# The first weights are loaded on another queue, and the list schedule is given other durations

## The chip, the cores and the metric

The kernel runs on one core of a Trainium2 chip. The metric is the time of one execution on the device, in microseconds (us); lower is better.

## What is computed

Sliding-window attention (window 64) on 4 batches of 8 heads, 576 positions and 64 dimensions, then two gated layers on the resulting 2304 tokens of 512 features. The weights are float64, everything else float32.

```python
scores = where(0 <= i - j < 64, q @ k.T / sqrt(64), -1e9)
x = softmax(scores) @ v               # 2304 tokens x 512
h = x @ w_in                          # 512 -> 2048
x = (h * clip(h + 3, 0, 6) / 6) @ w_out
h = x @ w2_in
out = leaky_relu(h, 0.01) @ w2_out    # 2304 x 512
```

## The kernel before

TensorE (PE) does every product. For the two layers each operand is split into a high and a low part, and three matmuls (high·high, high·low, low·high) add up in one PSUM bank, so a block of 128 x 512 costs three matmuls. The tokens are cut into five blocks (four of 512, one of 256), the hidden 2048 features into 16 slices of 128, f. For every (layer, block, f), `st_h` makes `h` (line 576; 12 matmuls) and `st_y` adds its product with the second weight to the four banks `y` (line 635; 12 matmuls).

**Weights.** `convert` brings one piece of weights (128 rows of 512 float64 values, 512 KB) into `st` and makes two tiles of it, `w0h`/`w0l` (first weight) or `w1h`/`w1l` (second). ScalarE (ACT) writes the absolute value `ca` (line 343) and the scaled low word `cr` (354); VectorE (DVE) clamps and shifts `ca` in two steps (331), puts sign and exponent back (350), adds `cr` (304); ACT copies the sum to the high tile (294) and DVE subtracts for the low tile (304). That is five DVE operations and three ACT operations for each of 64 pieces.

**Attention.** 20 items, each one or two query blocks. `st_S` writes the mask into the banks `y` (early items) or `a` by a matmul with the identity (line 453) and adds the products of `kt` and `qt` (466). DVE takes the maximum (`nb`, 425 and 426), ACT the exponentials (`s`, 414), DVE sums and inverts (435, 421, 422), GpSimd (POOL) scales (305). `st_P` transposes on PE (483, into banks `h`), ACT copies (`pt`), `st_V` multiplies by `v` (514), ACT copies into `xa`. The first 512-token block needs nine items before its first `h`; its tokens are then split by ACT into `xs0h`..`xs3h` and by DVE into `xs0l`..`xs3l`.

**What sets the order.** The kernel first records every operation with the engines that could do it, a duration for each, and what it reads and writes. `Order.run` then plays list scheduling forward and backward six times, keeps the shortest plan and issues the operations in its order. Durations come from the helpers `act`, `dve`, `pool` and `pe`, DMAs from `load`; every load is issued on the queue of SyncE (SP). Outside that list stands a preamble: `zero` (DVE memset, and an ACT activation that brings in the table for exp), the identity `ident_r` and the mask `mask_r`, made by POOL in a buffer and cast by DVE (lines 674 and 685). The list does not hold these, though line 453 needs both. The engines run their own instructions strictly in order, and wait for each other by semaphores.

Of the kernel before, what the change touches and what calls it, by code (L numbers as in the profile page):

```python
# [10 lines left out]
U32 = mybir.dt.uint32  # L11
# [204 lines left out]
def swa_relu6_leaky_kernel(ctx: ExitStack, tc: tile.TileContext, q, k, v, w_in, w_out, w2_in, w2_out, out):  # L216
# [14 lines left out]
    nc = tc.nc  # L231
    B, _, NP, S = k.shape
    NT, DM = out.shape
    DFF = w_out.shape[0]
    P = 128
# [9 lines left out]
    SCALE = 1.0 / float(DM // (2 * NP)) ** 0.5  # L245
    MASKED = -(2.0 ** 30)
    APART = lambda n, e: n < 5
    EARLY = 9

    blocks = [(sum(SIZES[:i]), n) for i, n in enumerate(SIZES)]  # L250
# [22 lines left out]
    op = od.op  # L273
# [8 lines left out]
        return ("ACT", 0.19 + n * 0.00083, fn)  # L282

    def dve(n, fn, fast=False):
        return ("DVE", 0.15 + n * (0.00052 if fast else 0.00104), fn)

    def pool(n, fn):
        return ("POOL", 0.2 + n * 0.0024, fn)

    def pe(t, fn):  # L290
        return ("PE", t, fn)
# [13 lines left out]
        p = pool(n, lambda: nc.gpsimd.tensor_tensor(out=dst(), in0=a(), in1=b(), op=alu))  # L305
        return (d, p) if last else (p, d)

    def load(bytes_, dst, src, writes):
        op([("SP", 0.62, lambda: nc.sync.dma_start(out=dst(), in_=src))], writes=writes)  # L309
        op([("DMA", bytes_ / 3.6e5, lambda: None)], writes=writes, delay=2.0)  # L310


# [2 lines left out]
    parts = {}  # L315

    def convert(layer, f, part):
        src = ((w_in, w_out), (w2_in, w2_out))[layer][part]
        st = buf("st", [P, DM, 2], U32, bufs=3)
        a = buf("ca", [P, DM], U32)  # L320
        r = buf("cr", [P, DM], U32)
        hi = buf(f"w{part}h", [P, DM], F32R, bufs=RING)
        lo = buf(f"w{part}l", [P, DM], F32R, bufs=RING)
        parts[layer, f, part] = hi, lo
        load(
            P * DM * 8, lambda: st().rearrange("p n t -> p (n t)"),
            src[f * P:(f + 1) * P, :].bitcast(U32), [st],
        )

        def ts(dst, src, s1, s2, op0, op1=None):  # L330
            return dve(DM, lambda: nc.vector.tensor_scalar(  # L331
                out=dst(), in0=src(), scalar1=s1, scalar2=s2, op0=op0, **({"op1": op1} if op1 else {})
            ), True)

        def high():
            return st()[:, :, 1]

        def af():
            return a().bitcast(F32)


        op([
            act(DM, lambda: nc.scalar.activation(out=af(), in_=high().bitcast(F32), func=AF.Abs)),
            ts(a, high, 0x7FFFFFFF, None, ALU.bitwise_and),
        ], [st], [a])
        op([ts(af, af, EXP_LO, EXP_HI, ALU.max, ALU.min)], [a], [a])

        op([ts(a, a, 3, 0x3FFFFFFF, ALU.logical_shift_left, ALU.bitwise_and)], [a], [a])

        op([dve(DM, lambda: nc.vector.scalar_tensor_tensor(  # L350
            out=a(), in0=high(), scalar=0xC0000000, in1=a(), op0=ALU.bitwise_and, op1=ALU.bitwise_or
        ))], [a, st], [a])

        op([act(DM, lambda: nc.scalar.activation(
            out=r(), in_=st()[:, :, 0], func=AF.Copy, scale=2.0 ** -29
        ))], [st], [r])
        op(tensor_tensor(DM, a, a, r, ALU.add, ADD_BY_VECTOR), [a, r], [a])
        op(copy(DM, hi, af, True), [a], [hi])
        op(tensor_tensor(DM, lo, af, lambda: hi().bitcast(F32), ALU.subtract), [a, hi], [lo])
# [83 lines left out]
    def st_S(n, pps):  # L443
        b, us = items[n]
        t = (us[0] - 1) // 2 if us[0] else 0
        if (b, t) not in tiles:
            load_tile(b, t)
        x, y = tiles[b, t]
        L = P if us[0] else W

        early = n < EARLY
        for pp in pps if early else ():
            op([pe(0.25, lambda pp=pp: nc.tensor.matmul(
                pp()[:, 0:NP * L].rearrange("p (c l) -> p c l", c=NP), ident_r,
                mask_r[:, P - L:P].unsqueeze(1).to_broadcast([P, NP, L]), start=True, stop=True,
                skip_group_check=True,
            ))], writes=[pp])

        def fn():
            for c in range(NP):  # L460
                for e in range(2):
                    r = slice(e * W, (e + 1) * W)
                    for j in range(len(us)):
                        part, pp = (j, pps[e]) if us[0] else (e, pps[0])
                        i = j + (1 if us[0] and not t else 0)
                        nc.tensor.matmul(  # L466
                            pp()[part * W:(part + 1) * W, c * L:(c + 1) * L], y()[r, i, c, :],
                            x()[r, c, j * W:j * W + L], start=not early,
                            stop=True, skip_group_check=early,
                        )  # L470

        op([pe(0.25 + NP * 0.222 * L / P, fn)], [x, y], pps)
        probs[n] = [softmax(L, pp, early, early and APART(n, e)) for e, pp in enumerate(pps)]

    def st_P(n, pps):
        L = P if items[n][1][0] else W
        pts[n] = []
        for (s, sv), pp in zip(probs.pop(n), pps):
            pt = buf("pt", [P, NP * P], bufs=3)

            def fn(sv=sv, pp=pp):
                for c in range(NP):
                    nc.tensor.transpose(pp()[0:L, c * P:(c + 1) * P], sv()[:, c, :], ident)  # L483

            op([pe(NP * 0.11, fn)], [s], [pp])
            op(copy(NP * P, lambda pt=pt: pt()[0:L], lambda pp=pp: pp()[0:L]), [pp], [pt])
            pts[n].append(pt)

# [10 lines left out]
    def st_V(n, po):  # L499
        b, us = items[n]  # L500
        L = P if us[0] else W
        pt = pts.pop(n)
        vs = []
        for i in us:
            vv = od.slot("v", sb, [P, DM], F32, 2, HOMES["v"])
            load(L * DM * 4, lambda vv=vv: vv()[0:L], v[b, (i + 1) * W - L:(i + 1) * W, :], [vv])
            vs.append(vv)

        def fn():
            for j, vv in enumerate(vs):  # L510
                for c in range(NP):
                    for e in range(2):
                        x, i = (pt[e], j) if us[0] else (pt[0], e)
                        nc.tensor.matmul(  # L514
                            po()[e * W:(e + 1) * W, (j * NP + c) * W:(j * NP + c + 1) * W],
                            vv()[0:L, (2 * c + e) * W:(2 * c + e + 1) * W],
                            x()[0:L, c * P + i * W:c * P + (i + 1) * W], start=True, stop=True,
                        )

        op([pe(0.15 + len(us) * NP * 0.125, fn)], [*vs, *pt], [po])  # L520
        n0 = b * NQ + us[0]
        bb, o = block_of(n0 * W)
        if len(us) == 2 and block_of((n0 + 1) * W)[0] != bb:
            groups = [((0,), bb, o), ((1,), *block_of((n0 + 1) * W))]
        else:
            groups = [(tuple(range(len(us))), bb, o)]
        for js, bb, o in groups:
            m = len(js)
            op(copy(
                m * NP * W,  # L530
                lambda bb=bb, o=o, m=m: xa[bb].rearrange("p (c l) -> p c l", c=NK)[:, :, o:o + m * W].rearrange(
                    "p c (j w) -> p j c w", j=m),
                lambda js=js, m=m: po()[:, js[0] * NP * W:(js[0] + m) * NP * W].rearrange(
                    "p (j c w) -> p j c w", j=m, c=NP),
            ), [po], [("x", n0 + j) for j in js])
# [18 lines left out]
    gs, xs, ys = {}, {}, {}  # L554
# [7 lines left out]
    def st_h(idx):  # L562
        layer, b, f, first, last = steps[idx]
        n = blocks[b][1]
        if first:
            names = x_names(layer, b)
            src = xb if layer else xa
            for c in range(NK):
                xs[c] = split(n, f"xs{c}", lambda c=c: xc(src, b, c), [names[c]] if layer else names)
        hi, lo = parts[layer, f, 0]  # L570
        ph = bank("h", 2)
        for c in range(NK):
            def fn(c=c, x=xs[c]):
                cs = slice(c * P, (c + 1) * P)
                for m, (wt, xt) in enumerate(((hi, x[0]), (lo, x[0]), (hi, x[1]))):
                    nc.tensor.matmul(  # L576
                        ph()[:, 0:n], wt()[:, cs], xt()[:, 0:n],
                        start=(c == 0 and m == 0), stop=(c == NK - 1 and m == 2),
                    )
            op([pe(3 * (0.0132 + n / 2400), fn)], [hi, lo, *xs[c]], [ph])  # L580
        r = buf("r", [P, 512])
        gh = buf("gh", [P, 512], F32R)
        gl = buf("gl", [P, 512], F32R)
# [10 lines left out]
        if layer == 0:  # L594
# [3 lines left out]
                    out=rr(), in0=h(), scalar1=3.0, scalar2=0.0, op0=ALU.add, op1=ALU.max  # L598
# [18 lines left out]
    def st_y(idx):  # L617
        layer, b, f, first, last = steps[idx]
        o, n = blocks[b]
        hi, lo = parts[layer, f, 1]  # L620
        gh, gl = gs.pop(idx)
        for c in range(NK if layer == 0 else n // P):
# [13 lines left out]
                        y()[:, 0:wide], stat, mov, start=(first and m == 0), stop=(last and m == 2)  # L636
                    )

            op([pe(3 * (0.0132 + wide / 2400), fn)], [hi, lo, gh, gl], [y])
            if last:  # L640
                if layer == 0:
                    def dst(c=c):
                        return xc(xb, b, c)
# [148 lines left out]
```

## Time and profile before

| | |
|---|---|
| three runs, median | 880.3 us (880.25 to 880.75) |
| profiled execution, its own time | 880.97 us |
| its span, first to last instruction | 879.1 us |
| PE busy | 865.7 us (98%) |
| DVE busy | 532.1 us (61%) |
| ACT busy | 450.8 us (51%) |
| POOL busy | 39.8 us (5%) |

The profile gives, for one execution, what each engine did when, and for each idle stretch what ended it. A stretch of time can be asked for by itself, which matters here: the shares above are means over a start in which five engines work on attention and on weights, and a long rest in which PE does little but matmuls. "Granted clock" (PEclk) is that of TensorE; DMA is the busy share of the core's 16 DMA engines.

### The profile page before, as it was taken

How to read it: one execution, taken by the hardware profiler on the slowest of the kernel's cores; microseconds unless marked ns; L12 is line 12 of the kernel's file. 1: busy time of each engine (PE TensorE's matmuls, PEld its weight loads, DVE VectorE, ACT ScalarE, POOL GpSimd, SP SyncE). 2: the span in 40 equal slices, each digit the busy share in tenths (PEclk: the TensorE clock that was granted, in tenths of full speed). 3: DMA queues.
4: the chain of work that ended last, by engine and by line, in shares of the span. 5: the costliest groups of instructions: out<-in, count | busy, mean ns of one | idle time of the engine just before them, and what ended most of it. 6: DMA issues, size and time to landing. Idle time of an engine off the chain costs nothing.

```text
span 879.1 us, 13163 instructions
## 1 busy us (share of the span) xinstructions
PE 865.7 (98%) x5056; PEld 719.9 (82%) x5056; DVE 532.1 (61%) x1113; ACT 450.8 (51%) x982; POOL 39.8 (5%) x45
## 2 busy tenths in 40 slices
PE   8899999999999999999999999999999999999998
PEld 6677777888988888888889888888888888888887
DVE  6999745443788345886337863233887346744344
ACT  6988866554666233664325663244765234433322
POOL 2221211110000000000000000000000000000000
PEclk9999999999999999999999999999999999999999
DMA  9864542100233000221001320000232000011011
GB/s 305 264 217 153 165 139 66 40 22 1 72 101 116 1 0 8 90 96 49 1 0 48 112 81 1 1 0 1 97 120 73 0 1 25 1 49 48 1 48 72
DMA packets 27551, 59.05 MB, mean 67 GB/s; under 512 B 2400, under 2 KB 10592, under 8 KB 27488
## 3 DMA queue, kind: packets, MB, share of 16 engines
q1 hardware_dynamic: 27488, 58.21, 20.3%
q8 instruction: 40, 0.66, 0.3%
q14 instruction: 23, 0.19, 0.1%
HBM read 53.48 MB, written 4.72 MB: 66 GB/s over the span
## 4 chain that ended last, share of the span: by engine, by line
PE 93%; DVE 4%; ACT 1%; DMA 1%; issue 1%; SPq 0%; POOL 0%; ACTq 0%; POOLq 0%; DVEq 0%
PE y L635 44%; PE h L576 44%; PE a L514 2%; PE a L466 1%; PE a L483 1%; DMA st<-in_moe_w_in_dram 1%; DVE nb L425 1%; PE h L483 0%; DVE ca L350 0%; ACT s L414 0%; SPq L309 0%; DVE w1l L304 0%; DVE ca L331 0%; DVE ca L304 0%; ACT pt L294 0%
## 5 line engine op out<-in xcount | busy, mean ns | idle before, releaser
L294 ACT ACTIVATE r<-h 128x512 f32<-128x512 f32 (+1 forms) x80 | 44.4, 554 | 161.9 <-PE h L576 161.6
L294 ACT ACTIVATE gh<-r 128x512 fp32r<-128x512 f32 (+1 forms) x160 | 93.9, 587 | 63.8 <-DVE r L610 35.4
L610 DVE SCALAR_TENSOR_TENSOR r<-r 128x512 f32<-128x512 f32 (+1 forms) x80 | 51.0, 638 | 114.8 <-ACT r L294 114.5
L635 PE MATMUL y<-gh,w1h 128*128 128x512 f32 (+1 forms) x320 | 119.8, 374 | 0.0
L635 PE MATMUL y<-gl,w1h 128*128 128x512 f32 (+1 forms) x320 | 118.2, 370 | 0.0
L635 PE MATMUL y<-gh,w1l 128*128 128x512 f32 (+1 forms) x320 | 118.1, 369 | 0.0
L635 PE MATMUL y<-w1l,gh 128*128 128x512 f32 x288 | 112.4, 390 | 0.0
L635 PE MATMUL y<-w1h,gh 128*128 128x512 f32 x288 | 112.4, 390 | 0.0
L635 PE MATMUL y<-w1h,gl 128*128 128x512 f32 x288 | 112.2, 389 | 0.0
L596 ACT ACTIVATE r<-h 128x512 f32<-128x512 f32 (+1 forms) x80 | 44.1, 553 | 120.0 <-PE h L576 119.6
L601 DVE SCALAR_TENSOR_TENSOR r<-r,h 128x512 f32<-128x512 f32 (+1 forms) x80 | 50.5, 633 | 84.0 <-ACT r L596 83.9
L635 PEld LDWEIGHTS y<-gh,w1h 128*128 128x128 f32 x320 | 60.4, 189 | 10.7 <-issue 0.9
L635 PEld LDWEIGHTS y<-gl,w1h 128*128 128x128 f32 x320 | 60.4, 189 | 10.5 <-DVE gl L605 0.3
L635 PEld LDWEIGHTS y<-gh,w1l 128*128 128x128 f32 x320 | 60.4, 189 | 9.6
L304 DVE TENSOR_TENSOR gl<-r,gh 128x512 fp32r<-128x512 f32 (+1 forms) x80 | 51.0, 637 | 26.8 <-ACT gh L294 25.7
L605 DVE SCALAR_TENSOR_TENSOR gl<-r,gh 128x512 fp32r<-128x512 f32 (+1 forms) x80 | 53.0, 663 | 18.8 <-ACT gh L294 18.1
L635 PEld LDWEIGHTS y<-w1h,gl 128*128 128x128 f32 x288 | 54.1, 188 | 11.3
L635 PEld LDWEIGHTS y<-w1l,gh 128*128 128x128 f32 x288 | 54.2, 188 | 10.7
L635 PEld LDWEIGHTS y<-w1h,gh 128*128 128x128 f32 x288 | 54.1, 188 | 10.7
L576 PE MATMUL h<-xs0h,w0h 128*128 128x512 f32 (+1 forms) x160 | 60.4, 377 | 0.0
L576 PE MATMUL h<-xs0l,w0h 128*128 128x512 f32 (+1 forms) x160 | 59.1, 370 | 0.5 <-DVE xs0l L304 0.5
L576 PE MATMUL h<-xs3h,w0h 128*128 128x512 f32 (+1 forms) x160 | 59.6, 372 | 0.0
(101 smaller groups left out, 1771.8 us busy)
## 6 DMA issues: line engine op xcount, KB each, us to landing
st<-in_moe_w_in_dram SPq DMA_DIRECT2D x32, 512.0 KB, 3.5
st<-in_moe_w_out_dram SPq DMA_DIRECT2D x32, 512.0 KB, 3.4
out_dram<-xa SPq DMA_DIRECT2D x18, 256.0 KB, 2.0
v<-in_v_dram SPq DMA_DIRECT2D x16, 256.0 KB, 4.1
xb<-in_v_dram SPq DMA_DIRECT2D x16, 256.0 KB, 3.0
kt<-in_k_dram SPq DMA_DIRECT2D x8, 384.0 KB, 4.7
qt<-in_q_dram SPq DMA_DIRECT2D x12, 256.0 KB, 3.9
xb<-in_k_dram SPq DMA_DIRECT2D x8, 384.0 KB, 6.3
```

The source lines that it names most:

```text
L294: a = act(n, lambda: nc.scalar.activation(out=dst(), in_=src(), func=AF.Copy, scale=scale))
L304: d = dve(n, lambda: nc.vector.tensor_tensor(out=dst(), in0=a(), in1=b(), op=alu))
L425: nc.vector.tensor_reduce(out=nb(), in_=p3(), axis=AX.X, op=ALU.max)
L466: nc.tensor.matmul(pp()[part * W:(part + 1) * W, c * L:(c + 1) * L], y()[r, i, c, :], x()[r, c, j * W:j * W + L], start=not early, stop=Tr ...
L483: nc.tensor.transpose(pp()[0:L, c * P:(c + 1) * P], sv()[:, c, :], ident)
L514: nc.tensor.matmul(po()[e * W:(e + 1) * W, (j * NP + c) * W:(j * NP + c + 1) * W], vv()[0:L, (2 * c + e) * W:(2 * c + e + 1) * W], x()[0:L ...
L576: nc.tensor.matmul(ph()[:, 0:n], wt()[:, cs], xt()[:, 0:n], start=(c == 0 and m == 0), stop=(c == NK - 1 and m == 2),)
L596: act(n, lambda: nc.scalar.activation(out=rr(), in_=h(), func=AF.Relu, bias=3.0)),
L601: op([dve(n, lambda: nc.vector.scalar_tensor_tensor(out=rr(), in0=rr(), scalar=6.0, in1=h(), op0=ALU.min, op1=ALU.mult))], [r, ph], [r])
L605: op([dve(n, lambda: nc.vector.scalar_tensor_tensor(out=gl()[:, 0:n], in0=rr(), scalar=1.0 / 6.0, in1=gg().bitcast(F32), op0=ALU.mult, op1 ...
L610: op([dve(n, lambda: nc.vector.scalar_tensor_tensor(out=rr(), in0=rr(), scalar=0.01, in1=rr(), op0=ALU.mult, op1=ALU.max))], [r], [r])
L635: nc.tensor.matmul(y()[:, 0:wide], stat, mov, start=(first and m == 0), stop=(last and m == 2))
```

## The change

The first piece of weights is issued by ACT's queue instead of SP's (`AT_ONCE = 1`). The durations given to the scheduler change: fast DVE operations and plain ones get a larger fixed part, POOL a smaller rate, and the PE operations of the first four attention items a surcharge; PE operations get a delay of 0.17 to 0.25 between their end and their use.

```diff
+    AT_ONCE = 1
     def dve(n, fn, fast=False):
-        return ("DVE", 0.15 + n * (0.00052 if fast else 0.00104), fn)
+        return ("DVE", (0.19 if fast else 0.16) + n * (0.00052 if fast else 0.00104), fn)
     def pool(n, fn):
-        return ("POOL", 0.2 + n * 0.0024, fn)
+        return ("POOL", 0.2 + n * 0.0018, fn)
-    def load(bytes_, dst, src, writes):
-        op([("SP", 0.62, lambda: nc.sync.dma_start(out=dst(), in_=src))], writes=writes)
+    def load(bytes_, dst, src, writes, engine="SP"):
+        queue = nc.scalar if engine == "ACT" else nc.sync
+        op([(engine, 0.62, lambda: queue.dma_start(out=dst(), in_=src))], writes=writes)
-            src[f * P:(f + 1) * P, :].bitcast(U32), [st],
+            src[f * P:(f + 1) * P, :].bitcast(U32), [st], "ACT" if len(parts) <= AT_ONCE else "SP",
-        op([pe(0.25 + NP * 0.222 * L / P, fn)], [x, y], pps)
+        op([pe(0.25 + NP * 0.222 * L / P + (0.3 if n < 4 else 0.0), fn)], [x, y], pps, 0.2)
-            op([pe(NP * 0.11, fn)], [s], [pp])
+            op([pe(NP * 0.11 + (0.15 if n < 4 else 0.0), fn)], [s], [pp], 0.25)
-        op([pe(0.15 + len(us) * NP * 0.125, fn)], [*vs, *pt], [po])
+        op([pe(0.15 + len(us) * NP * 0.125, fn)], [*vs, *pt], [po], 0.2)
-            op([pe(3 * (0.0132 + n / 2400), fn)], [hi, lo, *xs[c]], [ph])
+            op([pe(3 * (0.0132 + n / 2400), fn)], [hi, lo, *xs[c]], [ph], 0.17)
-            op([pe(3 * (0.0132 + wide / 2400), fn)], [hi, lo, gh, gl], [y])
+            op([pe(3 * (0.0132 + wide / 2400), fn)], [hi, lo, gh, gl], [y], 0.17)
```

The numbers matter by the order they lead to. The lines of the changed kernel lie one or two higher than those of before.

ACT, from the start of the program, before and then now:

```order
L671 ACT_TABLE_LOAD
L671 ACTIVATE zero<-zero 128x1
L414 ACTIVATE s<-y_97,nb 128x64 x4
L414 ACTIVATE s<-y_99,nb 128x128 x4
L343 ACTIVATE ca<-st 128x512
L414 ACTIVATE s<-y_101,nb 128x128 x4
L354 ACTIVATE cr<-st 128x512
```

```order
L311 DMA st<-in_moe_w_in_dram 128x1024
L673 ACT_TABLE_LOAD
L673 ACTIVATE zero<-zero 128x1
L345 ACTIVATE ca<-st 128x512
L356 ACTIVATE cr<-st 128x512
L416 ACTIVATE s<-y_97,nb 128x64 x4
L295 ACTIVATE w0h<-ca 128x512
L416 ACTIVATE s<-y_101,nb 128x128 x4
```

The load stands ahead of the table load, and the first piece's `ca` and `cr` now stand ahead of the first exponentials instead of behind them.

DVE, from the start of the program (`ident_r` and `mask_r` are the preamble's casts, `nb` the first attention maxima), before and then now:

```order
L670 MEMSET zero 128x1
L674 CAST ident_r<-xb_71 128x128
L685 CAST mask_r<-xb_71 64x128 x2
L425 TENSOR_REDUCE nb<-y_97 128x4
L426 TENSOR_SCALAR nb<-nb 128x4
L425 TENSOR_REDUCE nb<-y_99 128x4
L426 TENSOR_SCALAR nb<-nb 128x4
L435 TENSOR_REDUCE sm<-s 128x4
```

```order
L672 MEMSET zero 128x1
L333 TENSOR_SCALAR ca<-ca 128x512 x2
L352 SCALAR_TENSOR_TENSOR ca<-st,ca 128x512
L676 CAST ident_r<-xb_71 128x128
L687 CAST mask_r<-xb_71 64x128 x2
L427 TENSOR_REDUCE nb<-y_97 128x4
L428 TENSOR_SCALAR nb<-nb 128x4
L305 ISA ca<-ca,cr 128x1024
L427 TENSOR_REDUCE nb<-y_101 128x4
```

Three operations on the first piece of weights now stand ahead of the casts of the identity and of the mask, and a fourth behind the first maximum.

SP, from the start of the program, before and then now:

```order
L309 DMA kt<-in_k_dram 128x4x192
L309 DMA qt<-in_q_dram 128x768
L309 DMA kt<-in_k_dram 128x4x192
L309 DMA qt<-in_q_dram 128x512
L309 DMA v<-in_v_dram 64x512
L309 DMA st<-in_moe_w_in_dram 128x1024
L309 DMA xb_74<-in_k_dram 128x4x192 x2
```

```order
L311 DMA kt<-in_k_dram 128x4x192
L311 DMA qt<-in_q_dram 128x768
L311 DMA kt<-in_k_dram 128x4x192
L311 DMA qt<-in_q_dram 128x512
L311 DMA st<-in_moe_w_out_dram 128x1024
L311 DMA v<-in_v_dram 64x512
L311 DMA xb_74<-in_k_dram 128x4x192
L311 DMA st<-in_moe_w_in_dram 128x1024
```

The second piece of weights takes the place that the first had, one place earlier, and a third stands among the first eight loads.

## Rows read from the trace of the kernel before

**Rows 1.** Page, parts 1 and 4: busy time by engine; the chain that ended last.

```profile
PE 865.7 (98%) x5056; PEld 719.9 (82%) x5056; DVE 532.1 (61%) x1113; ACT 450.8 (51%) x982; POOL 39.8 (5%) x45
PE 93%; DVE 4%; ACT 1%; DMA 1%; issue 1%; SPq 0%; POOL 0%; ACTq 0%; POOLq 0%; DVEq 0%
```

**Rows 2.** Busy time by stretch: columns in the first line.

```profile
core 0: us, PE busy (x) PEld busy (x) DVE busy (x) ACT busy (x) POOL busy (x), PEclk, DMA share, GB/s
10.00:36.00 26.00, 21.73 (x291) 16.73 (x283) 24.43 (x60) 22.66 (x59) 9.22 (x9) 0.93 0.97 331
36.00:66.00 30.00, 29.38 (x254) 22.53 (x254) 29.43 (x63) 26.41 (x87) 6.88 (x6) 1.00 0.67 215
66.00:86.00 20.00, 19.31 (x185) 15.21 (x184) 19.14 (x57) 17.64 (x44) 3.39 (x3) 1.00 0.52 164
```

**Rows 3.** Timeline of the start: start, length, engine, line, operation [idle before <-releaser].

```profile
2.04 0.45 DVE L685 CAST mask_r<-xb 64x128 fp32r<-64x128 f32 x2 [0.30 <-POOL xb L680]
2.54 1.86 PE L453 MATMUL y<-mask_r,ident_r 128*128 128x256 f32 x4 [2.54 <-DVE mask_r L685]
5.61 2.83 PE L466 MATMUL y<-kt,qt 64*64 64x64 f32 x48 [1.20 <-DMA qt<-in_q_dram]
6.77 0.42 DVE L425 TENSOR_REDUCE nb<-y 128x4 f32<-128x256 f32 x1 [4.28 <-PE y L466]
7.50 0.93 ACT L414 ACTIVATE s<-y,nb 128x64 f32<-128x64 f32 x4 [5.26 <-DVE nb L426]
8.46 0.69 DVE L425 TENSOR_REDUCE nb<-y 128x4 f32<-128x512 f32 x1 [1.06 <-PE y L466]
```

**Rows 4.** Chain of waits, to 70 us, in order of time: start, length, what.

```profile
3.93 6.99 DMA st<-in_moe_w_in_dram
10.92 0.02 issue
10.94 0.02 ACT ca L343
10.97 0.56 issue
11.53 1.11 ACT s L414 x4
```

**Rows 5.** Timeline: single operations that the sum is made of.

```profile
0.74 0.67 SPq L309 DMA_DIRECT2D kt<-in_k_dram  x1
1.44 0.29 DVE L674 CAST ident_r<-xb 128x128 fp32r<-128x128 f32 x1 [0.57 <-POOL xb masks.py:199]
10.94 0.68 ACT L343 ACTIVATE ca<-st 128x512 f32<-128x512 f32 x1 [0.35 <-DMA st<-in_moe_w_in_dram]
25.38 0.41 DVE L331 TENSOR_SCALAR ca<-ca 128x512 uint32<-128x512 uint32 x1
32.19 0.68 DVE L350 SCALAR_TENSOR_TENSOR ca<-st,ca 128x512 uint32<-128x512 uint32 x1
18.17 0.66 DVE L304 CUSTOM_DVE_ANT_0 ca<-ca,cr 128x1024 uint16<-128x1024 uint16 x1
```

**Rows 6.** Busy time by stretch of 1 us (columns as in rows 2).

```profile
2.00:3.00 1.00, 0.46 (x2) 0.46 (x3) 0.44 (x2) 0.22 (x2) 0.00 (x1) 1.00 0.60 115
3.00:4.00 1.00, 1.00 (x4) 0.59 (x3) 0.00 (x0) 0.00 (x0) 0.00 (x0) 1.00 1.04 355
4.00:5.00 1.00, 0.41 (x1) 0.00 (x0) 0.00 (x0) 0.00 (x0) 0.00 (x0) 1.00 1.04 345
5.00:6.00 1.00, 0.39 (x8) 0.42 (x10) 0.00 (x0) 0.00 (x0) 0.00 (x0) 1.00 0.89 245
```

**Rows 7.** DMA issues by line: count, KB each, median us to landing.

```profile
st<-in_moe_w_in_dram SPq DMA_DIRECT2D x32, 512.0 KB, 3.5
```

**Rows 8.** Busy time by stretch around the granted clock (columns as in rows 2).

```profile
2.50:18.40 15.90, 14.36 (x133) 10.52 (x137) 9.97 (x29) 8.46 (x27) 3.76 (x4) 1.00 1.03 337
18.40:28.60 10.20, 6.93 (x138) 5.37 (x130) 9.55 (x23) 9.39 (x27) 3.69 (x4) 1.00 1.06 367
28.60:32.20 3.60, 3.46 (x38) 3.25 (x38) 3.53 (x8) 2.68 (x6) 1.77 (x2) 0.53 0.82 274
```

**Rows 9.** Timeline: transposes of 128 columns before and after 18.4 us.

```profile
16.56 1.06 PE L483 MATMUL h<-ident_r,s 128*128 128x128 f32 x4
20.08 0.66 PE L483 MATMUL h<-ident_r,s 128*128 128x128 f32 x4
```

## The prediction

> **What bounds the kernel now.** I read the page's busy times and chain first. PE is busy 98% of the span and makes 93% of the chain that ended last [rows 1], so the end is set by PE, and a change can only move the time that PE loses. Then the busy time by stretch: from 36 us on PE idles 0.62 us in 30 and 0.69 in 20, and the pieces of the change that touch the later matmuls have almost nothing to win. In the start it loses more: 4.27 of 26 us between 10 and 36 [rows 2], besides the first 2.54 us in which it does nothing and a wait of 1.20 us for `qt` [rows 3]. What the reader is to see in the same rows is DVE: 24.43 of 26 us, 29.43 of 30, 19.14 of 20. Until 86 us DVE is as full as PE, idle 1.57, 0.57 and 0.86 us. It makes attention's maxima and every piece of weights. So through the first tenth of the run two engines are bounds at once, and **a microsecond by which DVE's stream slips is a microsecond by which the weights and `xs` reach PE later**, unless DVE has idle time to swallow it.
>
> The chain seems to say something else: it holds 6.99 us of the load of the first weights [rows 4], which is what the change shortens. But it is followed there into `ca` on ACT, then 0.56 us that wait for nothing shown, then the exponentials: the link is ACT's order, not a use of the weights. The first 10.9 us are named after a load that no attention operation needs.
>
> **The change, part by part.**
>
> *The load on ACT's queue.* ACT's next work with a deadline came at 7.50 after 5.26 us of idleness [rows 3], so an issue of some 0.67 us (as SP's first [rows 5]) ahead of the table load costs nothing there. On SP it takes one issue off the queue; `v`, now behind two pieces of weights instead of one, has attention's own delay (below) as its cover. When does the piece land? Issued at 0.74, with the median of 3.5 us [rows 7] it is there at 4.2; with the 6.99 us that it took before [rows 4] at 7.7. Between them I count bytes. The DMA engines moved 115, 355, 345 and 245 kB in the microseconds from 2 to 6 [rows 6], and their share is 1.04, so they are full. Were all of it `st` (524 kB), its last byte would come at 4.15; with half of it, at 5.95, since `kt` and `qt` are under way as well. From the last byte of `qt` (786 kB, at 4.9 by the same count) to the matmul that waited for it, at 5.61 [rows 3], there are 0.7 us. That makes 4.8 to 6.6; I take the middle, 5.7, and keep 4.2 and 7.7 as ends.
>
> The Trainium skill speaks against the change here: "DMA: Bandwidth & Descriptors", section "Issuing engines are not separate DMA queues", says that loads started by different engines run on the same 16 DMA engines and interleave, so a second queue saves only the issue time. The trace agrees as far as it can: with one queue the share is 1.04 already [rows 6].
>
> *The casts behind the weights.* This is the part that decides. On DVE the order puts two 331 and one 350 of the first piece ahead of the casts of the identity and the mask. The cast of the mask ended at 2.49 and released PE's first matmul at 2.54 [rows 3]. Now it waits for the landing, then for ACT's `ca` (0.68), two 331 (0.41 each), the 350 (0.68), the cast of the identity (0.29) [rows 5] and of the mask (0.45 [rows 3]): 2.92 us, and with five hand-offs of 0.05 (2.49 to 2.54) 3.2. PE starts at 5.7 + 3.2 = 8.9 (ends 7.4 and 10.9) instead of 2.54. Before, the products of the first item could have begun at 5.61 - 1.20 = 4.41 had `qt` been there, 1.87 after the first mask matmul. Now `qt` is there: the bytes of `st`, `kt` and `qt`, 1.31 MB, pass by about 7. So the products begin at 10.8 instead of 5.61: **5.2 us later (3.7 to 7.2)**, and the first maximum on DVE with them, at 11.9 instead of 6.77.
>
> *What DVE has gained by then.* Of the first piece it has done 0.41 + 0.41 + 0.68 = 1.50 us, in time that was idle (4.28 us ahead of the first maximum [rows 3]). The 304 that adds `cr`, 0.66 us [rows 5], stands behind the first maximum, where 1.06 us were idle [rows 3]. Together 2.16 us of DVE's work are out of the way. The slip of its stream is 5.2 - 2.16 = **3.0 us (1.5 to 5.0)**.
>
> *The new durations.* They change the order, not the work: no operation is added or dropped. Their best case is that the new order fills what DVE idles between 10 and 36: -1.57 us [rows 2]. I can't price it from one trace and take zero of it; the order now also puts more conversion ahead of the first `xs0l`, which delays the first `h` but is work that is needed later anyway. Beyond 86 us PE is dense before, and the different order there is worth nothing either way.
>
> *PE's pace in the start.* Four transposes took 1.06 us at 16.56 and 0.66 at 20.08 [rows 9], while the granted clock reads 1.00 in both stretches [rows 8]: until about 18.4 PE ran at little more than half its later pace. Its slow stretch began with its first matmul; if it is as long again (15.9 us), it now ends 6.3 us later. PE was busy 6.93 of 10.2 us after 18.4 [rows 8], which gives 4.3 us of its work in 6.3 us, and half as much again would be 2.1 us if nothing hid it. DVE, busy 9.55 of the same 10.2 us, hides most. Ends 0 and 2.1; I take 0.5, since DVE's row is the nearest bound.
>
> **The sum.** 3.0 + 0 + 0.5 = 3.5 us more than the profiled execution's 880.97 us, so 884.5. The median of the runs is 0.67 us under that execution, which gives **883.8 us**. By the ends: 1.5 - 1.6 + 0 = -0.1, so 880.2, and 5.0 + 2.1 = 7.1, so 887.4.
>
> **The rivals.**
>
> *Absorbed.* DVE's idle time swallows the slip: it lands early (4.8, a slip of 2.1) and the new order closes the 1.57 us; 880.3 + 0.5 = 880.8, and with the middle landing 881.7. For it: a plan whose durations lie nearer the real ones should leave fewer gaps. Against: DVE's gaps are mostly short hand-offs to ACT and PE, which no order removes. 0.20.
>
> *Faster.* The first weights, not attention, gate the first `h`, as the chain of waits would have it [rows 4]. Then the piece ready five microseconds earlier shortens the start, and PE gets back what it idled from 18.4 to 28.6, 10.2 - 6.93 = 3.3 us [rows 8]: 877.0. It decides if DVE's slip is under zero, that is if attention starts less than 2.16 us late, for which the piece would have to land 3 us earlier than I take it, before even the 4.2 of the median. Against it too: `ca` led only into ACT's exponentials. 0.07.
>
> *A lower clock.* The granted clock fell to 0.53 between 28.6 and 32.2 [rows 8], nearly the whole stretch at the lower of the two levels (1.2 instead of 2.4 GHz), after 10 us in which PE idled a third. A start in which PE waits longer can repeat this: 3.46 us of PE's work at half pace are 1.7 us, with 2.1 instead of 0.5 for the slow start: 883.8 + 1.7 + 1.6 = 887.1. For it: PE's idle time moves to 2.5 to 8.9 and the slow stretch with it. Against: DVE sets the pace there. 0.13. The Trainium skill, "TensorE: Matmul & The Clock Gate", section "Part 1: The HAM clock gate", has the low clock as the state from which activity releases the engine, which fits the later rise; by it this rival's first part is certain, and its price is still what DVE leaves uncovered.
>
> *The load gains nothing.* ACT's queue shares with `kt` and `qt` so badly that the piece takes its 6.99 us again and lands at 7.7, and the casts still wait for it: 2.0 us more, 885.8. 0.10.
>
> **How the numbers follow.** The forecast has 0.50. A measurement of this kernel can tell about 0.2%, so 878.5 to 882.1 counts as the same. Slower: the forecast, the lower clock and the useless load, 0.50 + 0.13 + 0.10 = 0.73. Same: absorbed, 0.20. Faster: 0.07. The range runs from 881.0, inside the absorbed case, to 887.0, next to the lower clock and under the end of the sum at 887.4: out of it fall the faster case, the lower part of the absorbed one and the worst of the clock, some 0.2 together.
>
> **What would show it.** In the profile after, the timeline of the start should show the cast of the mask at about 8.4 with DVE's 331 and 350 ahead of it, PE's first matmul near 8.9, the first maximum near 11.9; the load on ACT should land between 4.8 and 6.6. DVE should be full from 12 to about 88, and PE dense as before beyond that: the whole difference must lie before 90 us. The forecast is wrong if the casts come before 4 us whatever the order says, if the first `h` comes no later than at 36 us, or if the time changes beyond 100 us.

## The result and the profile after

The changed kernel takes **886.54 us** (median of 4 runs, 885.98 to 887.04) against 880.34 us: a ratio of 1.0066 [1.0051, 1.0081], some 6.2 us slower by the medians and 5.8 by the ratio. The prediction said 883.8, 881.0 to 887.0, and slower. The profiled execution has a span of 884.9 us, 5.8 more than before.

The page of the kernel after, parts 1 and 4 (before: [rows 1]):

```profile
PE 864.2 (98%) x5056; PEld 718.4 (81%) x5056; DVE 534.9 (60%) x1113; ACT 452.2 (51%) x982; POOL 40.3 (5%) x45
PE 94%; DVE 4%; ACT 1%; issue 0%; DMA 0%; ACTq 0%; DVEq 0%
```

The same instructions run, and PE is even busy 1.5 us less, yet the span is longer, so PE waits more. Where, the busy time by stretch tells; first the kernel after, then the kernel before in the same stretches:

```profile
core 0: us, PE busy (x) PEld busy (x) DVE busy (x) ACT busy (x) POOL busy (x), PEclk, DMA share, GB/s
0.00:10.00 10.00, 2.35 (x14) 1.60 (x16) 2.09 (x7) 2.71 (x4) 1.37 (x9) 1.00 0.83 271
10.00:20.00 10.00, 8.34 (x113) 5.81 (x112) 8.59 (x25) 8.14 (x27) 2.65 (x3) 1.00 1.06 358
20.00:36.00 16.00, 11.97 (x187) 9.81 (x186) 15.62 (x35) 12.25 (x32) 7.07 (x6) 0.79 0.75 231
36.00:45.00 9.00, 6.75 (x86) 5.06 (x87) 7.99 (x19) 8.47 (x25) 0.61 (x1) 0.81 0.84 272
45.00:66.00 21.00, 19.58 (x182) 14.84 (x182) 19.66 (x42) 17.45 (x53) 4.70 (x4) 1.00 0.57 178
66.00:86.00 20.00, 20.00 (x149) 15.87 (x147) 17.71 (x50) 15.81 (x50) 4.71 (x4) 1.00 0.63 202
sum 86.00, PE 68.98 PEld 52.99 DVE 71.66 ACT 64.83 POOL 21.12; mean PE 11.50 PEld 8.83 DVE 11.94 ACT 10.80 POOL 3.52
```

```profile
0.00:10.00 10.00, 6.22 (x69) 4.59 (x73) 2.90 (x10) 2.96 (x9) 1.36 (x9) 1.00 0.77 225
10.00:20.00 10.00, 9.74 (x120) 7.36 (x112) 9.15 (x27) 8.48 (x24) 5.06 (x5) 1.00 1.07 370
20.00:36.00 16.00, 11.99 (x177) 9.37 (x173) 15.28 (x35) 14.17 (x35) 4.16 (x4) 0.89 0.91 307
36.00:45.00 9.00, 8.50 (x77) 6.24 (x77) 8.79 (x20) 8.61 (x33) 1.92 (x2) 1.00 0.60 184
45.00:66.00 21.00, 20.88 (x181) 16.29 (x177) 20.64 (x44) 17.80 (x55) 4.96 (x4) 1.00 0.71 229
sum 86.00, PE 76.64 PEld 59.06 DVE 75.90 ACT 69.67 POOL 20.85; mean PE 12.77 PEld 9.84 DVE 12.65 ACT 11.61 POOL 3.48
```

(The last stretch of before is in [rows 2].) In 86 us PE idles 17.02 us instead of 9.36, 7.7 more: 3.9 before 10 us, 1.4 from 10 to 20, 1.75 from 36 to 45, 1.3 from 45 to 66, and 0.7 less after that. The 1.5 us of shorter busy time leaves about 6.2, and 0.3 us less idle time beyond 106 us brings it near the 5.8 of the spans. **All of the loss lies before 66 us**, and half of it is not at the start. VectorE did not stay full either: from 10 to 86 us it idles 6.4 us instead of 3.0.

The start of the kernel after, from the timeline (before: [rows 3]); the first row is the load:

```profile
0.74 0.38 ACTq L311 DMA_DIRECT2D st<-in_moe_w_in_dram  x1
4.79 0.66 ACT L345 ACTIVATE ca<-st 128x512 f32<-128x512 f32 x1 [2.15 <-DMA st<-in_moe_w_in_dram]
5.48 0.89 DVE L333 TENSOR_SCALAR ca<-ca 128x512 f32<-128x512 f32 x2 [4.62 <-ACT ca L345]
6.41 0.69 DVE L352 SCALAR_TENSOR_TENSOR ca<-st,ca 128x512 uint32<-128x512 uint32 x1
7.15 0.45 DVE L687 CAST mask_r<-xb 64x128 fp32r<-64x128 f32 x2
7.65 1.86 PE L455 MATMUL y<-mask_r,ident_r 128*128 128x256 f32 x4 [7.65 <-DVE mask_r L687]
9.44 2.83 PE L468 MATMUL y<-kt,qt 64*64 64x64 f32 x48
10.61 0.42 DVE L427 TENSOR_REDUCE nb<-y 128x4 f32<-128x256 f32 x1 [3.01 <-PE y L468]
12.32 0.80 PE L455 MATMUL y<-mask_r,ident_r 128*128 128x512 f32 x1
14.50 0.49 PE L455 MATMUL y<-mask_r,ident_r 128*128 128x512 f32 x1
```

The mask's cast stands behind the first piece and PE starts at 7.65 instead of 2.54 (8.9 was forecast); the first maximum comes 3.84 us later. The last two rows show PE's pace: a mask matmul takes 0.80 us at 12.32 and 0.49 at 14.50, so the slow start is over by then, where before it lasted to about 18.4 [rows 9]. (The trace's record of the granted clock begins only where the pace has risen, at 13.64 us here and at 18.46 before; the 1.00 that the column shows ahead of that is not on record.)

Between 20 and 45 us the timeline has three places that the kernel before has not: VectorE's conversions (333, 352) ahead of maxima whose scores are done (PE had them at 21.03), ScalarE's copy `pt` behind twelve exponentials with PE waiting 3.03 us for it, and item 6's second mask and scores ahead of the first `h`. The two rows below are of the kernel before, where the first `h` came at 35.94, 7.4 us earlier, and the same scores stood behind it:

```profile
21.59 0.66 DVE L352 SCALAR_TENSOR_TENSOR ca<-st,ca 128x512 uint32<-128x512 uint32 x1
22.17 1.26 DVE L333 TENSOR_SCALAR ca<-ca 128x512 f32<-128x512 f32 x1
23.36 0.68 DVE L427 TENSOR_REDUCE nb<-y 128x4 f32<-128x512 f32 x1
24.33 3.21 ACT L416 ACTIVATE s<-y,nb 128x128 f32<-128x128 f32 x12 [1.82 <-DVE nb L428]
27.35 0.68 ACT L295 ACTIVATE pt<-h 128x512 f32<-128x512 f32 x1
28.09 1.01 PE L516 MATMUL a<-pt,xb 128*64 128x64 f32 x13 [3.03 <-ACT pt L295]
40.81 0.70 PE L455 MATMUL a<-mask_r,ident_r 128*128 128x512 f32 x1 [1.73 <-ACT s L416]
41.44 1.98 PE L468 MATMUL a<-kt,qt 64*64 64x128 f32 x32
43.35 0.79 PE L578 MATMUL h<-xs0h,w0h 128*128 128x512 f32 x1
```

```profile
35.94 0.51 PE L576 MATMUL h<-xs0h,w0h 128*128 128x512 f32 x1
37.85 1.10 PE L466 MATMUL a<-kt,qt 64*64 64x128 f32 x32
```

The granted clock is at its lower level (1.2 instead of 2.4 GHz) in two stretches, 10.3 us together, instead of one of 3.6 [rows 8]. Busy time by stretch, columns as above:

```profile
27.30:34.10 6.80, 6.01 (x62) 5.19 (x64) 6.67 (x14) 5.42 (x13) 4.70 (x4) 0.50 0.75 249
40.90:44.40 3.50, 3.50 (x36) 2.54 (x37) 2.75 (x8) 3.04 (x6) 0.61 (x1) 0.51 0.84 273
```

One thing said of the kernel before has to be put right: the first block needs five items (nine query blocks), not nine, before its first `h`.

### The profile page after: what moved, and what is told of

The parts are those of the page before. It is cut to its first block, busy times and chain, and to the rows that moved or that the text cites. A ratio compares the mean times of both kernels' runs of the same rounds, so it can differ in the third digit from the quotient of the medians.

```text
span 884.9 us, 13175 instructions
## 1 busy us (share of the span) xinstructions
PE 864.2 (98%) x5056; PEld 718.4 (81%) x5056; DVE 534.9 (60%) x1113; ACT 452.2 (51%) x982; POOL 40.3 (5%) x45
## 4 chain that ended last, share of the span: by engine, by line
PE 94%; DVE 4%; ACT 1%; issue 0%; DMA 0%; ACTq 0%; DVEq 0%
PE h L578 45%; PE y L637 44%; PE a L516 2%; PE a L468 2%; PE a L485 1%; DVE nb L427 1%; DVE sm L437 1%; DMA st<-in_moe_w_in_dram 0%; ACT s L416 0%; DVE ca L352 0%; DVE ca L333 0%; PE y L468 0%; DVE rc L423 0%; DVE w0l L305 0%; DVE nb L428 0%
## 5 line engine op out<-in xcount | busy, mean ns | idle before, releaser
L637 PEld LDWEIGHTS y<-gl,w1h 128*128 128x128 f32 x320 | 60.3, 188 | 10.3
L637 PEld LDWEIGHTS y<-w1l,gh 128*128 128x128 f32 x288 | 54.1, 188 | 10.3
L333 DVE TENSOR_SCALAR ca<-ca 128x512 uint32<-128x512 uint32 (+1 forms) x128 | 56.2, 447 | 9.4 <-ACT ca L345 7.8
L578 PE MATMUL h<-xs0h,w0l 128*128 128x512 f32 (+1 forms) x160 | 59.2, 370 | 1.4 <-DVE w0l L305 1.4
L578 PE MATMUL h<-xs1h,w0h 128*128 128x512 f32 (+1 forms) x160 | 60.1, 375 | 0.0
```

Source lines behind the costliest of these rows:

```text
L333: return dve(DM, lambda: nc.vector.tensor_scalar(out=dst(), in0=src(), scalar1=s1, scalar2=s2, op0=op0, **({"op1": op1} if op1 else {})), ...
L578: nc.tensor.matmul(ph()[:, 0:n], wt()[:, cs], xt()[:, 0:n], start=(c == 0 and m == 0), stop=(c == NK - 1 and m == 2),)
L637: nc.tensor.matmul(y()[:, 0:wide], stat, mov, start=(first and m == 0), stop=(last and m == 2))
```

## The experiments

Twelve kernels. They ran on several chips, and each ratio is against the kernel before on the same chip; in square brackets stands its 95% interval. Microseconds by ratio are the ratio less one, times 881. The diffs show the lines that matter; `...` stands for lines left out. The casts at the head, and the late casts, are made by issuing the preamble inside the ordered program.

**The parts apart.** First the changed kernel with the casts of identity and mask at the head of VectorE's row; the load stays ScalarE's first instruction.

```diff
+        head = [i for i in rows if ops[i][0][used[i]][0] == "ACT"][:1] if ahead else []
+        for i in head:
+            ops[i][0][used[i]][2]()
+        pre()
...
```

> The changed kernel with one thing put back: the casts of the identity and of the mask stand at the head of DVE again, ahead of the operations on the first piece; ACT still issues the load first. Theory A (the casts behind the weights delay attention, and DVE, full until 86 us, passes that on): PE's first matmul is back near 2.5 us, the first maximum near 8.3 (the maximum stands behind three operations on the piece that landed at 4.8), and the time falls to 880 plus or minus 1.2. Theory B (the new durations made a worse order): it stays at 884 or more. Theory C (the lower clock of 10.2 us cost it): it falls only if the granted clock stays at 1.00 longer than in the changed kernel.

884.93 us, 1.0043 [1.0028, 1.0058]: 3.8 us slower than before, 2.0 better than the change, though the two intervals overlap. Theory A does not carry the whole: it asked for about 880. PE starts at 2.71, but its first products wait for `qt` longer than the 1.20 us of [rows 3], and the first maximum comes at 8.00 instead of 6.77. The timeline of PE:

```profile
2.71 1.86 PE L461 MATMUL y<-mask_r,ident_r 128*128 128x256 f32 x4 [2.71 <-DVE mask_r L694]
6.84 2.83 PE L474 MATMUL y<-kt,qt 64*64 64x64 f32 x48 [2.27 <-DMA qt<-in_q_dram]
21.28 1.10 PE L474 MATMUL y<-xb,qt 64*64 64x128 f32 x32 [0.45 <-DMA qt<-in_q_dram]
```

The same scores as in the last row, in the kernel before:

```profile
20.97 1.10 PE L466 MATMUL y<-xb,qt 64*64 64x128 f32 x32 [0.24 <-DMA qt<-in_q_dram]
```

The load on ScalarE's queue moves beside `qt`, and the first products come 1.2 us later for it. Early casts uncover the transfers: plainly at the very start, hardly at 21 us (0.45 us instead of 0.24). The Trainium skill, "DMA: Bandwidth & Descriptors", section "Issuing engines are not separate DMA queues", has loads of different engines interleave on the same 16 DMA engines; these rows agree: what `st` gained, `qt` paid.

The new durations alone, the load on SyncE:

```diff
-    AT_ONCE = 1
+    AT_ONCE = 0
```

> The new durations with every load on SP's queue. DVE starts with the casts as before. Theory A: within 1.2 us of before, 879 to 881.5. Theory B: most of the 6.2 us is here, 883 or more.

883.64 us, 1.0031 [1.0020, 1.0043], 2.7 us slower, with a start that hardly moves (first matmul at 2.54, first maximum at 7.07). The durations cost by themselves, by the order that they lead to. In the profiled execution the lower clock had some 10 us here, against less than 4 before, but that is not most of the price: the two runs with a mean granted clock of 0.998 took 883.03 and 883.80 us, the four of the kernel before at 0.998 on that chip 880.26 to 881.04.

The load alone (old durations), and the load with the casts first (as above):

```diff
-            src[f * P:(f + 1) * P, :].bitcast(U32), [st],
+            src[f * P:(f + 1) * P, :].bitcast(U32), [st], "ACT" if len(parts) <= 1 else "SP",
```

> The first load on ACT's queue with the old durations. The order again puts two 331 and one 350 of the first piece ahead of the casts. Theory A: PE's first matmul at about 7.6, first maximum at 10.6, time 883.5 to 887. Theory B: within 1.2 us of before.

> The first load on ACT's queue with the old durations, and the casts put back at DVE's head. If the late casts cost the same whatever the durations (they cost 1.6 us of the changed kernel's time, 886.5 to 884.9), it lands near 885. If the low clock from 29.1 to 42.7 us in the load-alone kernel was the consequence of the late start, it falls further, to 882 to 884.

886.82 us, 1.0065 [1.0050, 1.0080], and 884.08 us, 1.0032 [1.0019, 1.0044]. The load alone is as slow as the whole change: on top of it the new durations add next to nothing, though alone they cost 2.7. Of its 5.7 us the late casts are 2.9 (the two intervals don't overlap); the other 2.8 stay with early casts, where the products wait 2.26 us for `qt` as above and start at 6.83 instead of 5.61. What the rest of the 2.8 is was not followed.

Late casts without any load: the kernel before with 14 idle operations of VectorE on an unused buffer ahead of the casts.

```diff
...
+        nc.vector.memset(xb[1][:, 0:DM], 0.0)
+        for _ in range(13):
+            nc.vector.tensor_scalar(out=pad, in0=pad, scalar1=0x7FFFFFFF, scalar2=None, op0=ALU.bitwise_and)
```

> The kernel before, order unchanged, with a memset and 13 operations of 512 columns on an unused tile ahead of the casts on DVE (about 6 us), so that the mask is ready at about 7.5 as in the changed kernel, with no work of the list done meanwhile. Theory A: the first maximum comes 3.8 us later, at 10.6, and as nothing is gained by then the end moves by about the same, 884 to 886. If DVE's stream had room, under 881.5.

884.04 us, 1.0037 [1.0025, 1.0049]. The first maximum came at 10.94, 4.17 us late, and the run is 3.3 us longer (2.2 to 4.3): **about three quarters of a late start are paid** (half to all of it, by the interval).

**The clock.** The changed kernel with matmuls repeated where PE waits, with the same result:

```diff
+                for _ in range(9 if n == 6 and pp is pps[0] else 1):
...
-            for j, vv in enumerate(vs):
+            for j, vv in list(enumerate(vs)) * (4 if n == 1 else 1):
```

> The changed kernel, in which PE repeats matmuls whose result stays the same, in the two waits after which the granted clock fell: the products with v of item 1 four times (about 3 us from 24 on), a mask nine times (about 1.8 us from 38.6 on). Order and other engines unchanged. Theory C: the granted clock stays at 1.00 from 14 to the end, PE's work in the 10.2 us at half pace gets back up to 4 us of which DVE hides a part: 883 to 885.5. If DVE hides all of it: within 0.8 us of 886.5.

885.56 us, 1.0047 [1.0032, 1.0062]: a gain of 1.0 us by the medians and 1.7 by the ratios, which the intervals don't separate; in the traces the last matmul starts at 879.81 instead of 880.80. The stretch shows what was wanted, a clock that does not fall before 45 us (its record begins at 13.60):

```profile
10.00:45.00 35.00, 29.42 (x490) 23.06 (x487) 32.95 (x78) 29.46 (x86) 10.34 (x10) 1.00 0.90 284
```

**Which step of the order?** Three theories, none of which held. First: conversion work ahead of `xs0l` is paid in full. ScalarE's and VectorE's conversions from the fourth piece on are held back until the first block's last split is issued (`held` goes through the planned order and puts the marked operations, with what depends on them, behind a goal):

```diff
...
+        for i in rows:
+            _, deps, behind, _ = self.ops[i]
+            if waiting is not None and (i in self.hold or late & set(deps) or late & set(behind)):
+                late.add(i)
+                waiting.append(i)
+                continue
+            out.append(i)
...
```

> The changed kernel, in which ACT's and DVE's operations on the fourth and later pieces of weights are issued only after the last split of the first block (xs3l). Theory D: in all kernels so far PE loses about 10 us after its first h (9.95 to 11.06) and what differs is lost before it; weights converted ahead of xs0l (23 operations, 15.9 us, against 18 and 12.8 before) are paid in full. Then the first h comes 2 to 3 us earlier, near 41, and the time falls to 883.5 to 885. Theory A alone (only the late casts count): same as the changed kernel, 886 to 887, as PE waits for these weights later.

> Casts first and the fourth and later pieces held back: both at once. Theory D and A together: the gains add, 1.6 + 2 to 3 us off the changed kernel, 881.5 to 883; if the loss after the first h grows instead, 884 to 885.5.

893.62 us, 1.0135 [1.0120, 1.0150], and with the casts first 892.81 us, 1.0128 [1.0113, 1.0143]. The first `h` stayed at 43.26, though VectorE had eight operations less before `xs0l` (15 on weights instead of 23). Busy time by stretch, the first of the two:

```profile
36.00:42.00 6.00, 4.16 (x49) 3.36 (x49) 1.58 (x4) 3.38 (x14) 0.00 (x0) 0.72 0.68 221
```

Timeline of VectorE in the same kernel:

```profile
39.69 0.42 DVE L448 TENSOR_REDUCE nb<-a 128x4 f32<-128x256 f32 x1 [3.30 <-PE a L489]
```

VectorE idles 4.4 of 6 us, 3.3 of them waiting for PE and the rest for ScalarE: with its work away, attention's hand-offs bound the start. The held work was then missing later.

Second: PE's row. Item 6's second mask and its scores are held behind the first three matmuls of `h`, in the changed kernel and in the one with the casts first:

```diff
+            if n == 6 and pp is pps[1]:
+                od.hold.add(len(od.ops))
...
+            if idx == 0 and c == 0:
+                od.goal = len(od.ops)
```

> The changed kernel; on TensorE alone the second mask matmul and the scores of item 6 stand behind the first three matmuls of the first h, as they do in the kernel before, and no other engine's row is moved. Theory A (TensorE's new row is part of the price): the first h can start when xs0h is written (39.57 us in the trace of after) and not at 43.35, the third waits for xs0l (41.29), then the mask and the scores follow; about 1.0 us of matmuls falls into the wait for ScalarE that ended at 40.81, so 885.3 to 886.1 against 886.5. Rival B (the row of TensorE is without weight, since what ends late is the attention's chain on ScalarE and VectorE, which xs1l, written at 42.49, still follows): within 0.3 us of after. Rival C: item 6's maxima come later and the next items with them: slower than after by 0.5 us or more.

> The changed kernel with the casts of identity and mask at the head of VectorE's row (as in the run that moved the casts alone, 884.9) and with TensorE's row before the first h as in the run above. Theory A: both gains add, 883.7 to 884.6. Rival B: 884.9, as with the casts alone.

886.82 us, 1.0057 [1.0037, 1.0077], and 886.09 us, 1.0047 [1.0033, 1.0061]. Against the kernels without the move (886.54 and 1.0066, 884.93 and 1.0043) the medians show no gain; the first ratio is 0.8 us lower, which theory A asked for, the second is not, and the trace decides: the first `h` starts at 39.49 instead of 43.35, and 9 us later nothing is left of it. Timeline of the first of the two, then one row of the changed kernel:

```profile
39.49 0.50 PE L595 MATMUL h<-xs0h,w0h 128*128 128x512 f32 x1 [0.53 <-ACT xs0h L310]
41.22 0.50 PE L595 MATMUL h<-xs0l,w0h 128*128 128x512 f32 x1 [0.99 <-DVE xs0l L320]
41.88 1.72 PE L485 MATMUL a<-kt,qt 64*64 64x128 f32 x32
48.04 0.60 PE L502 MATMUL a<-ident_r,s 128*64 128x128 f32 x4
```

```profile
48.04 0.60 PE L485 MATMUL a<-ident_r,s 128*64 128x128 f32 x4
```

PE waits for `xs0l`, does the scores and the next matmuls at the lower clock, which now comes 1.3 us later, and reaches the next transposes at the same 48.04; the last matmul starts at 880.80 in both. Theory A fell, rival B held.

Third: ScalarE's wait for the load in the kernel with the durations alone, where the first `ca` stands ahead of ready exponentials. It is held behind them.

```diff
+        if len(parts) == 1:
+            od.hold.add(len(od.ops))
...
+            if od.item == 1:
+                od.goal = len(od.ops)
```

> The kernel before with the new durations alone (its load on SP, 883.6), and one step moved: ScalarE's first step of the first piece, which stood ahead of the exponentials of item 1 and waited 2.76 us for the load, is issued behind them; VectorE's first step of that piece, which reads it, moves with it. Theory D (an in-order engine that waits for a load while ready work stands behind it is what the new durations cost): the exponentials start at about 9.7 us and not at 12.06, later maxima, transposes and the first h follow by up to 2 us, 881.4 to 882.6. Rival E (the order further on costs it, the steps of weights between the attention's steps at 20 to 36 us): under 0.5 us gained, 883.1 to 883.8.

885.52 us, 1.0045 [1.0033, 1.0058], no better than 1.0031 without the edit, and slower than either theory had it. The timelines, first with the durations alone, then with the exponentials first:

```profile
11.49 0.66 ACT L345 ACTIVATE ca<-st 128x512 f32<-128x512 f32 x1 [2.76 <-DMA st<-in_moe_w_in_dram]
12.06 2.16 ACT L416 ACTIVATE s<-y,nb 128x128 f32<-128x128 f32 x8
19.83 1.10 PE L468 MATMUL y<-xb,qt 64*64 64x128 f32 x32
```

```profile
9.48 2.26 ACT L434 ACTIVATE s<-y,nb 128x128 f32<-128x128 f32 x8 [1.02 <-DVE nb L446]
19.58 1.98 PE L488 MATMUL y<-xb,qt 64*64 64x128 f32 x32 [0.83 <-DMA qt<-in_q_dram]
```

The exponentials start 2.6 us earlier, but the next scores only 0.25 us: they wait for `qt`. And they then run at the lower clock, 1.98 us instead of 1.10.

**The best with both parts of the change.** Casts first, `h` first, and repeated matmuls:

> The second of these kernels with matmuls repeated where TensorE waits, with the same result (the products of item 1 with its values four times, the first mask matmul of item 6 four times), which kept the granted clock at full speed from 13.6 us on when the changed kernel had them. Theory F (time at the lower clock counts about 1 us of every 10): 0.5 to 1.2 us below the second kernel, 882.6 to 883.9. Rival G (the time at the lower clock lies in waits once the casts are early, and the repeats cost their own 0.3 us each): no faster than it.

884.13 us, 1.0034 [1.0022, 1.0046], against 886.09 and 1.0047 without the repeats on the same chip: 2.0 us by the medians, more than theory F's 1.2, and 1.1 by the ratios, within it. Two of the eleven runs without them had a granted clock of 1.000 by themselves, and took 883.65 and 883.88: the repeats buy what a full clock is worth and no more. Nor is the clock the rest of the price: at a mean granted clock of 1.000 four of its runs took 883.93 to 884.01 us, three of the kernel before 880.02 to 880.70. No version beats the kernel before.

## Why the prediction was right, and where it was off

**Right.** The bound: PE's waits in the start decide, and a start that slips is mostly paid. The casts behind the weights: VectorE's 331, 331 and 350 (now 333, 333, 352) stood ahead of them as read from the order. The late casts' price, 3.0 us forecast, was 2.0 to 2.9 in the two pairs that differ in the casts, and 3.3 in the kernel with late casts alone. Next to nothing changed beyond 100 us; it was over by 66.

That 3.0 came near is in part luck. The working passed on the whole of a slip and took off 2.16 us of VectorE's work done meanwhile. With the measured 3.84 us that gives 1.7, less than was paid, and for the late casts alone, with no work done meanwhile, 4.2, where 3.3 were paid. The sign that VectorE would be full from 12 to 88 us did not come either (idle from 10 to 86 us: 6.4 us, 4.0 with the late casts alone, 3.0 before): VectorE waits more for the other engines than the working had.

**The step that failed: "I can't price it from one trace and take zero of it".** The new durations alone cost 2.7 us, as much as the 2.7 by which the median missed the forecast. The working named only a gain as their other end (-1.57), so the bound was open on the side where the result lay. That a plan with durations nearer the real ones "should leave fewer gaps" was an argument without a row; the rows between 20 and 45 us show new gaps. But the durations are not the only term put at nothing, and the parts do not add up: the load alone costs 5.7, all that was measured, of which the working had the late casts and not the transfers (below). Which of the two zeros is blamed hangs on the order in which the parts are put in.

**Over-sized: the landing.** 5.7 us was taken; it landed 4.03 us after its issue, by 4.77, just under the bracket's lower end of 4.8. With it the first maximum came 3.84 us late, not 5.2. It came as early as the end of the count that gave `st` all the bytes moved from 2 us on (4.15 and 0.7); with early casts `qt` is seen to come later for it.

**Missing: the displaced transfers.** The second piece of weights and the load on another queue were set to nothing because late attention covers them. That cover is there for the first products of the changed kernel, which wait for the mask and not for `qt`; with early casts it is gone, and the load costs 2.8 us with old durations and some 1.1 (3.8 less 2.7) with the new.

**Wrong in sign: PE's slow start.** It was to end 6.3 us later; it ended 4 to 6 us earlier, though PE started 5.1 us later. PE worked some 8.5 us less at half pace for it, and 6 us more in the low stretches; half of the difference is about the 1.5 us of busy time that it has less. Nor is it shown to come from the change. Two kernels with casts first (without and with `h` first), whose instructions come in the same order until 38 us, differ as much in their traces, in the mask matmul behind the first products:

```profile
9.71 0.79 PE L461 MATMUL y<-mask_r,ident_r 128*128 128x512 f32 x1
9.87 0.51 PE L478 MATMUL y<-mask_r,ident_r 128*128 128x512 f32 x1
```

The pace rose at 19.6 us in the first trace and by 9.9 in the second. (The end of 2.1 us was also small by its own rows: 1.06 against 0.66 us makes 2.6 of the 4.3 us of work.)

**The lower clock.** The rival's stretch came, nearly three times as long as before, at a price of 1.0 to 1.7 us by the run that keeps the clock up (1.8 by the line in the last section, for 6.7 us more at the lower level). That is about the 1.7 that the rival put on it; the 1.6 that it put on a longer slow start did not come. Its time was the nearest to the result (887.1), but for reasons that were not its own.

Put together by ratios: late casts 2.0, durations 2.7, the load's transfers 1.1, 5.8 in all. It is a subtraction of four kernels in a row, in which each has an interval of 1.0 to 1.3 us either way. By the other row, with the load put in before the durations, it is 2.8 for the transfers, 2.9 for the late casts and 0.1 for the durations. That the durations alone, the late casts alone, and the load with early casts each cost more than nothing is shown; the split is not.

**Open:** which steps of the new order cost the 2.7 us. Conversions ahead of `xs0l`, PE's row before the first `h`, and ScalarE's early wait each fell when tried, the first two in the changed kernel and not in the one with the durations alone. In the trace of the latter most of the price (2.4 us by the spans) lies up to `xs0l`: from the end of item 4's scores (22.07 before, 22.83 with the durations alone) to `xs0l` (36.43 and 38.32) 14.4 us became 15.5, and 0.8 us were lost ahead of that. A sum of short hand-offs fits; it was not shown.

## What to carry to other kernels

Instructions that stand outside a planner's list (here two casts) are late by whatever the planner puts ahead of them; look for them in each engine's row before anything else. A change of a planner's durations is a change of order, and its price has to be bounded on both sides. A load moved to another queue can be paid by the loads beside it, as `qt` paid here, so ask who waits for those. And prices of parts measured alone need not add up: here 5.7 and 2.7 made 5.8.

## What the hardware showed that was not expected

**Time at the lower clock is cheap here.** In 26 runs of the kernel before on one chip the mean granted clock went from 1.000 (880.02 us) to 0.992 (884.87 us). A line through them gives 0.27 us for each microsecond at the lower level (worked out as twice the missing share of 880 us); the eleven runs with casts and `h` first give the same 0.27, those with casts, `h` and repeats 0.21, the ten with the exponentials first 0.05, the seven with the durations alone 0.06. These are lines through runs as they fell, an estimate, and no run here changes the clock alone. A PE that bounded everything in such a stretch would lose 0.5.

**They fall at different times in kernels with the same order.** With casts first the first low stretch was at 29.8 to 33.3 us; with `h` moved at 38 us, at 20.1 to 23.5, long before the edit, where the scores took 1.91 us instead of 1.10. Each has a second one, at about 40 to 44.

**The slow start's length isn't fixed.** Before, PE kept half its pace for 15.9 us from its first matmul, busy 14.36 of them [rows 8]; in the kernel after the pace rose between 4.7 and 6.9 us after the first matmul, with next to no gap of PE until then. The mask matmul's 0.80 us there is what a matmul of 512 columns takes in the low stretches (0.79 at 43.35). Busy time by stretch of the kernel after:

```profile
7.65:13.60 5.95, 5.90 (x65) 4.31 (x69) 2.44 (x7) 1.74 (x7) 0.00 (x0) 1.00 1.06 332
```
